# Attention outputs split at query 240 with merged pieces, normalising on VectorE only, the loads of the first batches reordered and one estimate of the kernel's planner raised, in a fused attention and expert kernel

## The chip, the cores and the metric

One core of one Trainium2 chip. The metric is the time of one execution in microseconds, from a timer outside the profile. A profiled execution's span is about 1.7 us shorter than its time. A single-core run carries its mean granted TensorE clock as a share of full speed. A run more than 1.5% above the fastest of its kernel is marked slow and left out of ratios; where one is shown here, it says so.

## The reference, cut to what matters

Eight batches of eight heads, 576 queries, head size 64, with 16 "beacon" keys and values ahead of the 576 causal ones. The attention output, as 4608 tokens of 512, goes through one dense expert.

```python
k_all = np.concatenate([beacon_k, k], axis=2)          # 592 keys
v_all = np.concatenate([beacon_v, v], axis=2)
scores = scale * np.matmul(q, k_all.transpose(0, 1, 3, 2))
scores = np.where(causal, -1e9, scores)                # beacons always visible
a = np.exp(scores - scores.max(-1, keepdims=True))
a /= a.sum(-1, keepdims=True) + 1e-09
x = np.matmul(a, v_all)  # -> (4608, 512)
h = x @ w_in                                           # 512 -> 2048
g = h * (1.0 / (1.0 + np.exp(-1.702 * h)))
out = g @ w_out                                        # 2048 -> 512
```

## The kernel before

The kernel works through 32 attention steps (a pair of heads of one batch; four steps a batch) and nine groups of 512 tokens for the expert. Between attention steps TensorE does expert matmuls, which fill what would be waits for exp on ScalarE. Scores are held with keys on partitions and queries in columns, so the causal part of each of the five key tiles is a rectangle of columns, stored in four chunks:

```python
CH = [[(0, 0, 512)],
      [(0, 512, S), (2, s0s[2], S), (4, s0s[4], S)],
      [(1, s0s[1], S)],
      [(3, s0s[3], S)]]
```

The output of a head is made in two halves of the queries, split at `HS = 288`, each accumulated over key tiles in pieces that follow the chunks:

```python
def av_list(x, half):
    qa, qe = half * HS, (half + 1) * HS
    return [(j, lo - qa, hi - qa, col) for j in range(NJ)
            for (lo, hi, col) in e_pieces(j, max(qa, s0s[j]), qe)]
```

Half of each value tile holds ones, so the sums of exp come out beside the output. After the two copies of a head out of the tiles that TensorE writes (`O<-u`), VectorE transposes the sums (`zt<-O`, one for each head), takes the reciprocal, transposes it back (`rz<-rt`) and multiplies (`xT<-O,rz`, one for each head).

The order of every engine's instructions is computed in the kernel's own Python. Each piece of work carries an estimated duration, for one engine or for a choice of several. A greedy loop repeatedly takes the work that could start earliest by those estimates, picks the engine that would finish it first, and appends it. What comes out is the order of every engine's program. The estimates are typed in by hand:

```python
evs.append(Work(dict(DVE=0.45, ACT=0.46), 0, i + 0.5, ... av_out ...))
zn.append(Work("DVE", 0.68, i + 0.48, lambda i=i, x=x: z_turn(i, x), evs[-2:], ...))   # zt<-O
zr = Work("DVE", 0.2,  i + 0.45, ... z_recip ...)
zk = Work("DVE", 0.75, i + 0.45, ... z_back ...)
nw = Work(dict(DVE=0.78, POOL=1.42), 0, i + 0.45, ... norm ...)                        # xT<-O,rz
...
def issue():                       # cut
    while todo:
        for w in todo:             # skipped while what it needs is not placed
            t = max(end of what it needs + SEM, when its buffer is free)
            eng = min(w.opts, key=lambda e: max(t, free[e]) + w.opts[e] + ...)
            c = (max(t, free[eng]), 0 if same matmul mode else 1, w.key)
            # the smallest c is taken
        free[eng] = w.t0 + w.opts[eng]
        order.append(w)
```

Staging of q and k for batches 2 to 7 goes through two VectorE transposes (`sq<-n`), two copies on VectorE or GpSimd (`t<-sq`), and a pass through DRAM. Batches 0 and 1 are loaded and transposed on TensorE instead.

The softmax here doesn't subtract the row's maximum and nothing guards it: scores larger than these inputs give would overflow.

## Time and profile before

| | before |
|---|---|
| time, median of 3 (range) | 397.88 us (397.56 to 399.22) |
| span of the profiled run | 395.7 us |
| TensorE busy | 368.3 us, 93% |
| VectorE / ScalarE / GpSimd busy | 65% / 57% / 48% |
| five loaded periods (start of one first-expert group to the next) | 41.4, 45.3, 41.4, 42.7, 42.7 us |
| the unloaded period after them | 39.35 us |

The period is the most useful ruler in this kernel: apart from its start and its end it is a loop over batches, and the last of these periods, where nothing is left to stage, shows what the loop takes when TensorE is not kept waiting. From the table of instruction groups of the kernel before, besides what the prediction shows (columns: line, engine, operation, operands, count | busy us, mean ns | idle before them and what ended it):

```profile
L444 DVE STREAM_TRANSPOSE zt<-O 64x576 f32<-64x576 f32 x64 | 49.4, 772 | 1.9
L463 POOL TENSOR_TENSOR xT<-O,rz 64x576 f16<-64x576 f32 x24 | 40.8, 1701 | 71.6 <-DVE rz L454 71.5
L463 DVE TENSOR_TENSOR xT<-O,rz 64x576 f16<-64x576 f32 x40 | 48.8, 1220 | 0.7
```

Set these against the planner's estimates above. The sum transposes take 772 ns where the planner counts 680. The normalisations take 1701 ns on GpSimd (it counts 1420) and 1220 on VectorE (it counts 780). In the 24 pairs that both engines share, VectorE's took 750 ns in the 11 where it started first and 1.41 to 2.52 us in the 13 where GpSimd's did.

### The profile page before, as it was taken

What the parts mean: (1) busy time and instruction counts of PE and PEld (TensorE: products, weight loads), DVE (VectorE), ACT (ScalarE), POOL (GpSimd) and SP (SyncE); (2) the same over time, 40 slices, a digit from 0 to 9 for tenths busy, and PEclk for the clock granted to TensorE, in tenths of its full rate; (3) what the DMA queues carried; (4) which work ended last, traced back from release to release, by engine and by line L of the source; (5) the groups of instructions that cost most, each with busy time, mean ns of one, the idle gap of its engine ahead of it and who ended that gap; (6) DMA issues with size and microseconds to landing.
All of it is one profiled execution on the core that took longest, in us unless ns stands there. A gap on an engine that the chain in (4) does not pass through costs nothing.

```text
span 395.7 us, 6410 instructions
## 1 busy us (share of the span) xinstructions
PE 368.3 (93%) x2458; PEld 186.3 (47%) x2458; DVE 259.0 (65%) x425; ACT 227.3 (57%) x333; POOL 189.1 (48%) x282
## 2 busy tenths in 40 slices
PE   6997999989999799979997999979999999999996
PEld 3464544444544344534453774435454544444442
DVE  6469998699739973999469963997485349000021
ACT  1788766457674656656744766466658563644400
POOL 8664853469255854478337925584355044000000
PEclk9999999999999899999999899999999999999999
DMA  8999994849562795379346966279310010001022
GB/s 114 200 206 208 145 128 132 210 97 154 116 164 60 157 115 132 86 172 124 110 113 145 134 108 146 67 148 120 110 54 30 0 55 27 28 0 53 2 80 80
DMA packets 60894, 42.81 MB, mean 108 GB/s; under 512 B 32192, under 2 KB 53184, under 8 KB 60864
## 3 DMA queue, kind: packets, MB, share of 16 engines
q0 software_dynamic: 42816, 18.62, 38.8%
q1 hardware_dynamic: 18048, 23.79, 18.9%
q8 instruction: 19, 0.31, 0.3%
q14 instruction: 11, 0.09, 0.1%
HBM read 44.40 MB, written 16.61 MB: 154 GB/s over the span
## 4 chain that ended last, share of the span: by engine, by line
PE 50%; DVE 21%; DMA 5%; ACT 4%; issue 2%; POOL 2%; POOLq 1%; DVEq 0%; ACTq 0%
PE u L490 29%; PE u L512 13%; DMA n<-in_k_dram 5%; PE u L421 5%; DVE zt L444 4%; DVE O L432 4%; DVE xT L463 4%; DVE sq L275 4%; PE s L351 2%; ACT E L364 2%; ACT L364 2%; DVE rz L454 2%; DVE t L284 2%; POOL xT L463 1%; POOL t L284 1%
## 5 line engine op out<-in xcount | busy, mean ns | idle before, releaser
L490 PE MATMUL u<-xT,w 128*128 128x512 f16 (+1 forms) x640 | 133.7, 361 | 3.9 <-DVE O L432 1.6
L364 ACT ACTIVATE E<-s 128x1024 f16<-128x1024 f32 (+3 forms) x128 | 104.6, 873 | 49.2 <-PE s L351 45.5
L512 PE MATMUL u<-w,g 128*128 128x512 f16 x576 | 129.4, 379 | 2.3 <-DVE O L432 2.1
L502 ACT ACTIVATE g<-u 128x512 f16<-128x512 f32 x144 | 85.1, 597 | 59.6 <-PE u L490 59.3
L490 PEld LDWEIGHTS <-w 128*128 128x128 f16 x640 | 60.4, 99 | 62.7 <-issue 8.3
L512 PEld LDWEIGHTS <-g 128*128 128x128 f16 x576 | 54.8, 98 | 67.5 <-issue 3.4
L387 POOL TENSOR_SCALAR_AFFINE_SELECT E<-E 128x256 f16<-128x256 f16 (+2 forms) x144 | 58.6, 425 | 42.1 <-ACT E L364 40.8
L463 POOL TENSOR_TENSOR xT<-O,rz 64x576 f16<-64x576 f32 x24 | 40.8, 1701 | 71.6 <-DVE rz L454 71.5
L525 DVE COPY osb<-u 128x512 f32<-128x512 f32 x26 | 17.7, 681 | 76.9 <-PE u L512 76.8
L421 PE MATMUL u<-E,vb 128*128 128x288 f16 (+6 forms) x576 | 58.2, 246 | 7.8 <-POOL E L387 5.7
L432 DVE COPY O<-u 128x288 f32<-128x288 f32 x109 | 45.8, 442 | 27.0 <-PE u L421 26.5
L421 PEld LDWEIGHTS <-vb 128*128 128x128 f16 (+1 forms) x576 | 44.0, 98 | 25.6 <-issue 14.6
L444 DVE STREAM_TRANSPOSE zt<-O 64x576 f32<-64x576 f32 x64 | 49.4, 772 | 1.9
L463 DVE TENSOR_TENSOR xT<-O,rz 64x576 f16<-64x576 f32 x40 | 48.8, 1220 | 0.7
L351 PE MATMUL s<-qT,kT 64*128 64x80 f16 (+5 forms) x384 | 39.9, 286 | 6.1 <-ACT E L364 4.6
L284 POOL COPY t<-sq 128x576 f16<-128x576 f16 x22 | 30.7, 1397 | 26.6 <-DVE sq L275 26.6
L275 DVE STREAM_TRANSPOSE sq<-n 128x576 f16<-128x576 f16 x48 | 35.7, 755 | 4.4 <-DMA n<-in_k_dram 3.8
L351 PEld LDWEIGHTS <-kT 64*128 64x128 f16 x384 | 14.5, 94 | 32.6 <-issue 26.5
L454 DVE STREAM_TRANSPOSE rz<-rt 128x576 f32<-128x576 f32 x32 | 24.4, 762 | 1.3 <-DVE t L290 0.4
L243 POOL DMA_DIRECT2D vb<-in_v_dram x24 | 20.8, 873 | 0.0
L284 DVE COPY t<-sq 128x576 f16<-128x576 f16 x26 | 19.7, 757 | 0.5
L523 ACT COPY osb<-u 128x512 f32<-128x512 f32 x10 | 5.9, 588 | 17.0 <-PE u L512 17.0
(50 smaller groups left out, 147.0 us busy)
## 6 DMA issues: line engine op xcount, KB each, us to landing
out_dram<-osb SPq DMA_DIRECT2D x36, 256.0 KB
d<-t SPq DMA_DIRECT2D x24, 148.0 KB
kT<-d SPq DMA_DIRECT2D x12, 296.0 KB
n<-in_k_dram POOLq DMA_DIRECT2D x12, 288.0 KB, 5.3
n<-in_q_dram POOLq DMA_DIRECT2D x12, 288.0 KB, 6.2
d<-t SPq DMA_DIRECT2D x24, 144.0 KB
qT<-d SPq DMA_DIRECT2D x12, 288.0 KB
vb<-in_v_dram POOLq DMA_DIRECT2D x18, 128.0 KB, 5.5
```

Source lines behind the costliest of these rows:

```text
L275: nc.vector.transpose(sqs[(b, g, w)][:, c * n : (c + 1) * n, :, :], nat[(b, g, w)][:, c * n : (c + 1) * n, :],)
L284: copy[eng](out=tqk[(b, g, w)][:, e, o : o + S].rearrange("p (r t) -> p r t", t=TPP), in_=sqs[(b, g, w)][:, :, e, :].rearrange("p t r -> p ...
L351: nc.tensor.matmul(sc[:, x, o : o + e - a], kT[r : r + 64, p, j * P : (j + 1) * P], qT[r : r + 64, p, a:e], start=True, stop=True,)
L364: nc.scalar.activation(out=Es[i][:, :, choff[ci] : choff[ci] + w], in_=scs[(i, ci)][:, :, 0:w], func=AFT.Exp, scale=0.125,)
L387: nc.gpsimd.affine_select(out=blk, in_=blk, compare_op=ALU.is_ge, fill=0.0, base=mc, pattern=[[0, 2], [1, w]], channel_multiplier=-1,)
L421: nc.tensor.matmul(u[:, lo:hi], vb[0:kw, j, :, :].rearrange("r h c -> r (h c)")[:, o : o + 2 * D], E[0:kw, x, col : col + hi - lo], start= ...
L432: copy[eng](out=Os[i][:, x, half * HS : (half + 1) * HS], in_=avu[(i, x, half)][:, :])
L444: nc.vector.transpose(zst[i][0][64 * x : 64 * x + 64, :, :], Os[i][64 * (1 - x) : 64 * (1 - x) + 64, x, :])
L463: vec[eng].tensor_tensor(out=xT[r : r + 64, p, c : c + S], in0=Os[i][r : r + 64, x, :], in1=zst[i][2][r : r + 64, :], op=ALU.mult,)
L490: nc.tensor.matmul(u[:, o : o + w], w1t[:, kp, nt * P : (nt + 1) * P], xT[:, kp, m : m + w], start=(kp == 0), stop=(kp == NKP - 1),)
L502: nc.scalar.activation(out=gts[g][:, nt, :], in_=hu[(g, nt)][:, :], func=AFT.Gelu_apprx_sigmoid)
L512: nc.tensor.matmul(o[:, :], gts[g][:, nt, mt * P : (mt + 1) * P], w2t[:, nt, :], start=(nt == 0), stop=(nt == NNT - 1),)
```

## The change

The intent: fewer output matmuls (seven pieces a head instead of nine, by a split at query 240, where a chunk boundary of the keys falls, and by merging pieces that lie side by side), no normalising on GpSimd, which takes 1701 ns for one and beside which VectorE's took up to 2.52 us, and earlier loads of v. One more line raises a planner estimate (0.68 to 0.74 for the transpose of the sums). The diff, cut to its core:

```diff
-    HS = S // 2
+    HS = 2 * P - Nb
+    AQ = (0, HS, S)
+    NBV = 2
@@ e_pieces: merge neighbours
-            if lo < hi:
+            if lo < hi and got and got[-1][1] == lo and got[-1][2] + lo - got[-1][0] == col + lo - qa:
+                got[-1] = (got[-1][0], hi, got[-1][2])
+            elif lo < hi:
                 got.append((lo, hi, col + lo - qa))
@@ av_list, av_half, av_out: AQ[half : half + 2] in place of half * HS ...
@@ the first loads (cut)
-    mkeep = Work("POOL", 0.3, 0.0, make_keep)
+    mkeep = Work("POOL", 0.3, -4.75, make_keep)
-        lv = Work("POOL", 0.8, kl + 0.2, lambda b=b: load_v6(b), dma=3.6)
+    def first_values(b):
+        lv = Work("POOL", 0.8, -4.8, lambda b=b: load_v6(b), dma=3.6)
-                            Work("POOL", 0.6, 4.3, lambda x=x: load_bk(x), [V[1, 0]], dma=0.7)
+                            Work("POOL", 0.6, 4.3, lambda x=x: load_bk(x), after=[ld_], dma=0.7)
-            [vpe[NJ - 1], vpe[2 * NJ - 1]][c > 0 :][:1] if c < 3 else [], dma=3.0,
+            vpe[-1:] if 2 * c < 3 * NBV else [], dma=3.0,
+            after=[Lq[(2, 1, 0)]],
@@ the planner's buffer rings: qT, kT, vb as two rings of one instead of one ring of two (cut)
@@ the sum transpose
-                "DVE", 0.68, i + 0.48, lambda i=i, x=x: z_turn(i, x), evs[-2:],
+                "DVE", 0.74, i + 0.48, lambda i=i, x=x: z_turn(i, x), evs[-2:],
@@ the normalisation
-                dict(DVE=0.78, POOL=1.42), 0, i + 0.45, lambda eng, i=i, x=x: norm(i, x, eng),
+                dict(DVE=0.78), 0, i + 0.45, lambda eng, i=i, x=x: norm(i, x, eng),
```

More of the change, by code (lines that the diff above doesn't have):

```diff
@@ L81 @@
     bkn = cst.tile([Nb, NB2, H, D], F16, tag="bkn", name="bkn")
-    bvn = cst.tile([Nb, NB2, H, D], F16, tag="bvn", name="bvn")
+    bvn = cst.tile([Nb, NBV, H, D], F16, tag="bvn", name="bvn")
     def make_keep():
@@ L166, in load_beacons @@
             out=t.rearrange("n b h d -> n (b h) d"),
-            in_=src[0:NB2].rearrange("b h n d -> n (b h) d"),
+            in_=src[0 : t.shape[1]].rearrange("b h n d -> n (b h) d"),
         )
@@ L401, in av_list @@
     def av_list(x, half):
-        qa, qe = half * HS, (half + 1) * HS
+        qa, qe = AQ[half : half + 2]
         return [
@@ L413, in av_half @@
         E = Es[i]
-        u = psu.tile([P, HS], F32, tag="u", name="u")
+        u = psu.tile([P, AQ[half + 1] - AQ[half]], F32, tag="u", name="u")
         avu[(i, x, half)] = u
@@ L432, in av_out @@
         copy[eng](
-            out=Os[i][:, x, half * HS : (half + 1) * HS], in_=avu[(i, x, half)][:, :]
+            out=Os[i][:, x, AQ[half] : AQ[half + 1]], in_=avu[(i, x, half)][:, :]
         )
@@ L552 @@
     rings = dict(
-        n0=2, n1=2, sq=2, t0=2, t1=2, d0=4, d1=4, qT=2, kT=2, vb=2, s=2, E=2, u=4, O=3,
+        n0=2, n1=2, sq=2, t0=2, t1=2, d0=4, d1=4, qT0=1, qT1=1, kT0=1, kT1=1, vb0=1, vb1=1, s=2, E=2, u=4, O=3,
         zt=2, rt=2, rz=2, xT=RING, g=2, osb=3,
@@ L586, in first_loads @@
                     ))
-        lv = Work("POOL", 0.8, kl + 0.2, lambda b=b: load_v6(b), dma=3.6)
-        fb = []
         ub = Buf("u")
@@ L613, in first_loads @@
             kk = 4 * b + 0.5
-            x = Work("PE", 1.35, kk, lambda b=b, j=j: v_pe(b, j), [lv, mspread] + beac[1:], alloc=ub, after=vpe[-1:])
+            x = Work("PE", 1.35, kk, lambda b=b, j=j: v_pe(b, j), [lv, mspread] + beac[1:], alloc=ub,
+                after=vpe[-1:],
+            )
             V[(b, j)] = Work(
@@ L624 @@
     for b in range(B):
-        kTb[b], qTb[b], vbb[b], xTb[b] = Buf("kT"), Buf("qT"), Buf("vb"), Buf("xT")
+        kTb[b], qTb[b], vbb[b] = (Buf(f"{n}{b % 2}") for n in ("kT", "qT", "vb"))
+        xTb[b] = Buf("xT")
         bt = [qTb[b], kTb[b]]
@@ L628 @@
             first_loads(b)
-            continue
-        for g in range(2):
+        for g in range(2) if b >= NB2 else ():
             for w in (1, 0):
@@ L681 @@
                 placed[(b, g, w)] = pl
+        if b < NBV:
+            first_values(b)
+            continue
         for j in range(NJ):
             V[(b, j)] = Work(
-                "POOL", 0.9 + 0.6 * (j == 0), 4 * b - 1.5 + 0.1 * j,
+                "POOL", 0.9 + 0.6 * (j == 0), (4 * b - 1.5 if b >= NB2 else -3.9) + 0.1 * j,
                 lambda b=b, j=j: load_v(b, j, 0, H),
```

## The prediction

> **What bounds the kernel now.** I read the page's engine shares first, then the chain of work that ended last in order of time, then the windows of each stretch between two starts of the first expert matmul, then the waits, and last the timeline around the longest waits of TensorE.
>
> ```profile
> PE 368.3 (93%) x2458; PEld 186.3 (47%) x2458; DVE 259.0 (65%) x425; ACT 227.3 (57%) x333; POOL 189.1 (48%) x282
> ...
> PEclk9999999999999899999999899999999999999999
> ```
>
> TensorE is the bound, but 93% is flattering, since ends are modelled. [...] I took the starts of all matmuls from the trace and listed each gap that exceeds its own columns by over 0.25 us: 29 us, besides 4 us after the last matmul.
>
> ```profile
> 285.95 1.55 PE u L421 x18
> 287.50 0.55 PE s L351 x4
> 288.04 3.56 PE u L512 x16
> 291.60 0.53 PE s L351 x8
> 292.13 1.55 PE u L421 x18
> ```
>
> This is the chain in the seventh batch, where nothing is left to load: one attention step every 6.2 us, all TensorE. In the batches before it the chain leaves TensorE for VectorE and GpSimd. The first expert matmul of each group starts at 88.9, 134.2, 175.5, 218.3, 261.0 and 300.35 us (from the starts). So the periods are 45.3, 41.4, 42.7, 42.7, and 39.35 for the clean one; the period before 88.9 is 41.4. The same stretches as windows (columns: PE, PEld, DVE, ACT, POOL busy, clock, DMA share, GB/s):
>
> ```profile
> 89.00:134.00 45.00, 41.58 (x267) 20.68 (x265) 35.96 (x60) 27.11 (x39) 26.99 (x38) 0.97 0.69 134
> 134.00:175.50 41.50, 39.45 (x250) 19.11 (x248) 32.06 (x55) 26.12 (x38) 24.05 (x35) 0.99 0.66 121
> 175.50:218.30 42.80, 39.86 (x251) 19.16 (x250) 33.58 (x55) 26.50 (x38) 25.61 (x37) 0.98 0.68 127
> 218.30:261.00 42.70, 40.11 (x314) 25.86 (x313) 32.38 (x55) 26.01 (x38) 24.45 (x35) 0.98 0.65 119
> 261.00:300.30 39.30, 38.64 (x248) 18.89 (x246) 29.51 (x49) 24.99 (x38) 22.40 (x33) 1.00 0.50 97
> ```
>
> No other engine is full in any of them (VectorE 76 to 80%), so the 2 to 6 us a period are waits of order. Which ones:
>
> ```profile
> PE u L421 <- POOL E L387: 5.7, 4, 1.5
> ...
> PE s L351 <- ACT E L364: 4.6, 11, 0.5
> ```
>
> The first row is four waits, one a period: the output matmuls wait for a mask on GpSimd. Around one of them:
>
> ```profile
> 130.17 1.16 POOL L284 COPY t<-sq 128x576 f16<-128x576 f16 x1 [2.05 <-DVE sq L275]
> 131.27 0.74 POOL L387 TENSOR_SCALAR_AFFINE_SELECT E<-E 128x256 f16<-128x256 f16 x2
> 131.73 1.79 PE L421 MATMUL u<-E,vb 128*128 128x208 f16 x11 [1.46 <-POOL E L387]
> ```
>
> GpSimd stood 2.05 us waiting for VectorE's staging transpose, copied for 1.16 us, and only then masked what TensorE wanted. [...] The half-clock stretches in the trace (131.7 and 217.0, each 3.4 us) start right after two of these waits.
>
> [...]
>
> ```profile
> 123.78 1.40 POOL L463 TENSOR_TENSOR xT<-O,rz 64x576 f16<-64x576 f32 x1 [1.74 <-DVE rz L454]
> 123.90 1.90 DVE L463 TENSOR_TENSOR xT<-O,rz 64x576 f16<-64x576 f32 x1
> ...
> 334.96 0.75 DVE L463 TENSOR_TENSOR xT<-O,rz 64x576 f16<-64x576 f32 x1
> 335.05 0.81 PE L490 MATMUL u<-xT,w 128*128 128x512 f16 x3
> 335.07 1.90 POOL L463 TENSOR_TENSOR xT<-O,rz 64x576 f16<-64x576 f32 x1 [3.89 <-DVE rz L454]
> ...
> 337.02 0.38 PE L490 MATMUL u<-xT,w 128*128 128x512 f16 x1 [1.17 <-POOL xT L463]
> ```
>
> [...] the free ones here take 750.
>
> **The change part by part.**
>
> 1. Output matmuls. A head had 9 pieces (288, 176, 48; 224, 64, 288, 288, 208, 80 columns) and gets 7 (240, 128; 336, 336, 336, 208, 80); the columns stay 1664. So 128 matmuls go[...]: 0.6 us. [...] The removed quarter of the matmuls is worth next to nothing. The early part also no longer needs the third key tile.
>
> 2. Copies of the outputs. 109 copies of 288 at 0.442 us become 58 of 240 and 45 of 336 on VectorE. [...] these take 0.39 and 0.49 us: 44.8 us for 45.8 (x109 row, "O<-u 128x288"). Six move to ScalarE.
>
> 3. Normalising. 24 of 64 leave GpSimd (1701 ns each, 40.8 us). On VectorE they cost less than their count says. In 13 of the 24 pairs GpSimd was first, and VectorE's own half then took 1.4 to 2.5 us (sum 24.4), in 11 it was free (8.25): 32.6 us. The same pairs on VectorE alone take 24 x 1.51 = 36.2 us, so VectorE pays about 3.6 us in all, and each pair ends about 0.5 us sooner (2.0 to 1.5). Of this only the last pair is on the end's path for certain: 0.5 us.
>
> 4. The order, which moves because the schedule is computed from the part times. The instruction order shows it. In the four periods from 89 us the third step of each batch was torn (scores x2, 16 expert matmuls, scores x4, 3 output matmuls, scores x8, 15 output matmuls), with one staging copy on GpSimd between the masks of one step and another before the next. After, all steps have the pattern of the clean batch (16 expert, 8 scores, 14 outputs, 4 scores), and three of GpSimd's four copies a batch stand after the last mask of the batch. So the mask wait of 1.5 us, the 0.7 us score waits of the torn step and the half-clock stretches (up to 1.7 us each, two of them) should go. The waits that stay: 0.4 us after each table load, which the clean batch has too, and about 1 us behind a staging transpose that stands before three output copies on VectorE (117 us: it waits for its load). That load is issued some 0.7 us sooner without the normalisation ahead of it.
>
> 5. First loads. v of batch 1 goes ahead of its q and k, so these land some 2 to 3 us later (18.0 for the second before). They are first used at 22.6, so no wait. The queue of loads is unbroken to 57 us in both, with the same bytes. w_out comes later in issue but needs to be there at 65.9; I see it landing near 54. The batch-2 loads come some 4 us sooner. The mask constant leaves the end of GpSimd's first queue (VectorE waited 4.5 us for it, TensorE did not). I put the start at -0.5 us.
>
> Sum: five periods of 213.5 us together become five of 40.3, the clean 39.35 plus 0.95 for what stays of the staging waits: 201.5, so -12.0. Start -0.5, end -0.5; part 1 is mostly within the periods. Before 397.9, after near 385.
>
> **Rivals.** (a) VectorE takes the place of GpSimd as what TensorE waits for. A batch's steps with staging hold about 9 us of VectorE work (one 0.69 us output copy, 1.76 us of O copies, two transposes for the sums 1.55, reciprocal 0.25, transpose back 0.76, two norms 1.51, two staging transposes 1.5, a copy 0.76) against 6.2 us of TensorE, and only the first expert layer's stretch lets it catch up. For it: waits for O copies of about 1 us at 81.7 and 117. Against it: 32 to 34 us of work in a 40 us period, no more than before, since the blocked halves vanish. If it comes true the periods are 41 to 41.5 and the time 389 to 391. (b) Only the matmul count matters: then -0.6 us, 397. The torn step and its waits speak against it. (c) The gain goes through fully: periods as the clean one, both half-clock stretches gone, start better by 2: 379 to 381. (d) The late w_out or late q and k of batch 1 stall the start: +2 to +5 us there, visible as DMA waits; the landing times speak against it.
>
> **Range and chances.** I lean to the sum with a part of (a): 385.5, and 8 in 10 between 380.5 and 391.5. The 2% line is 389.9. Faster by over 2%: 0.77; within 2%: 0.21; slower: 0.02, since nothing but the start can lose time.
>
> **What would show it.** Right: the period starts 39.5 to 41 us apart; the wait of outputs for masks near zero; no normalisation on GpSimd, its busy time near 152 us; VectorE's 64 norms at about 0.8 to 0.9 us mean and its busy time 259 to 268; no half-clock stretch inside the periods; output matmuls' full step 1.52 us in the chain instead of 1.55. Wrong: new waits of TensorE for O copies of over 1.5 us a period (rival a), norms of 1.5 us blocked by GpSimd's copies, or DMA waits before 66 us.

## The result, and the profile after

The changed kernel took 385.22 us (median of 4, 382.18 to 386.69), the kernel before 397.99 us in the same rounds (397.56 to 399.22). The ratio is 0.9664, with a 95% interval of 0.9596 to 0.9733: faster by 3.4%. (A ratio here is the mean time of one kernel's fast runs over that of the other's of the same rounds, so not quite the ratio of the medians quoted.) All results agree with the reference.

The page of the changed kernel's profiled execution (386.69 us, the slowest of its four, granted clock 0.985):

```profile
PE 369.8 (96%) x2328; PEld 181.5 (47%) x2328; DVE 265.7 (69%) x443; ACT 226.3 (59%) x334; POOL 146.7 (38%) x263
...
PEclk9789899999999999999999999999999999999999
...
L467 DVE TENSOR_TENSOR xT<-O,rz 64x576 f16<-64x576 f32 x64 | 51.6, 807 | 0.8
```

TensorE's busy time is as before, though 130 matmuls fewer: what went is waiting. Sixty-four normalisations on VectorE take 51.6 us where forty took 48.8. The half-clock stretches (the granted clock is 0.5 in them) stood in the loop before, at 131.7 and 217.0 us; in this run they stand in the start, at 15.0 us (6.83 us long) and 38.9 us (3.41).

The stretches between the starts of the first expert matmuls, now 51.7, 93.9, 133.4, 172.6, 211.8, 251.3 and 290.6 us. The windows below begin with the second loaded period; the first took 42.18 us (columns as in the prediction):

```profile
93.90:133.40 39.50, 38.95 (x235) 18.49 (x234) 34.52 (x59) 25.93 (x38) 19.55 (x34) 1.00 0.72 135
133.40:172.60 39.20, 38.84 (x234) 18.35 (x233) 33.87 (x58) 25.76 (x38) 18.79 (x33) 1.00 0.73 133
172.60:211.80 39.20, 38.84 (x234) 18.42 (x232) 33.05 (x57) 25.76 (x38) 19.23 (x33) 1.00 0.74 134
211.80:251.30 39.50, 39.02 (x298) 24.67 (x296) 33.71 (x59) 25.84 (x38) 18.96 (x33) 1.00 0.75 133
251.30:290.60 39.30, 38.94 (x235) 18.41 (x234) 33.27 (x55) 25.67 (x39) 15.34 (x29) 1.00 0.54 110
```

The loaded periods are now as short as the unloaded one, with a full clock, although VectorE works 33 to 34.5 us in each (85%). Where the gain of the profiled run lies, from these starts:

| part | before | after | difference | predicted |
|---|---|---|---|---|
| start, to the first expert matmul | 47.49 | 51.73 | +4.24 | -0.5 |
| five loaded periods | 213.51 | 199.61 | -13.90 | -12.0 |
| the unloaded period and all after it | 134.70 | 133.66 | -1.04 | -0.5 |
| span | 395.7 | 385.0 | -10.7 | -13.0 |

The waits of TensorE in the changed kernel (engine, tile and line, what it waited for: us in total, times, longest):

```profile
PE s L355 <- ACT E L368: 2.5, 4, 1.0
...
PE u L516 <- DVE O L436: 1.7, 1, 1.7
```

The row "outputs wait for GpSimd's mask: 5.7, 4, 1.5" of before is gone. What replaced it is a single wait of 1.7 us, which ends at 81.4 us.

The chain in the seventh batch, to be held against the one before (outputs x18 in 1.55 us there):

```profile
281.84 0.53 PE s L355 x8
282.37 1.53 PE u L425 x14
283.90 0.56 PE s L355 x4
284.47 3.56 PE u L516 x16
```

Four matmuls fewer in a step shorten it by 0.02 us.

The order on TensorE, one loaded batch, from the traces (number of matmuls; expert1 and expert2 are the matmuls of the first and second expert layer, a bar stands between steps):

```
before: 16 expert2, 8 scores, 18 outputs, 2 scores | 16 expert2, 4 scores, 3 outputs, 8 scores, 15 outputs, 4 scores | 36 expert1 ...
after:  16 expert2, 8 scores, 14 outputs, 4 scores | 16 expert2, 8 scores, 14 outputs, 4 scores | 32 expert1 ...
```

The torn third step of the kernel before, on TensorE (start, us, engine, line, operation; in brackets the idle time before it and its releaser):

```profile
170.63 0.40 PE L421 MATMUL u<-E,vb 128*128 128x288 f16 x3
171.10 0.39 PE L351 MATMUL s<-qT,kT 64*128 64x64 f16 x6
172.01 0.37 PE L351 MATMUL s<-qT,kT 64*128 64x464 f16 x2 [0.53 <-ACT E L364]
172.32 0.54 PE L421 MATMUL u<-E,vb 128*128 128x224 f16 x4
174.19 1.01 PE L421 MATMUL u<-E,vb 128*128 128x208 f16 x11 [1.33 <-POOL E L387]
...
176.79 1.95 PE L490 MATMUL u<-xT,w 128*128 128x512 f16 x7 [0.43 <-DVE xT L463]
```

Outputs and scores alternate with no expert matmuls between them, so each waits for exp or for a mask: 2.3 us of waits in 8 us.

### The profile page after: what moved, and what is told of

Its sections match the earlier page's. It is cut to its first block, busy times and chain, and to the rows that moved or that the text cites.

```text
span 385.0 us, 6119 instructions
## 1 busy us (share of the span) xinstructions
PE 369.8 (96%) x2328; PEld 181.5 (47%) x2328; DVE 265.7 (69%) x443; ACT 226.3 (59%) x334; POOL 146.7 (38%) x263
## 4 chain that ended last, share of the span: by engine, by line
PE 55%; DVE 28%; ACT 7%; DMA 5%; issue 3%; POOL 0%; SPq 0%; ACTq 0%; DVEq 0%
PE u L494 28%; PE u L516 15%; DVE xT L467 6%; DVE zt L448 6%; DVE O L436 5%; PE u L425 5%; ACT E L368 4%; DMA n<-in_k_dram 3%; DVE sq L277 3%; PE s L355 3%; DVE rz L458 3%; PE u L216 2%; ACT L368 2%; PE u L916 2%; DVE osb L529 2%
## 5 line engine op out<-in xcount | busy, mean ns | idle before, releaser
L506 ACT ACTIVATE g<-u 128x512 f16<-128x512 f32 x144 | 83.9, 598 | 52.7 <-PE u L494 52.6
L529 DVE COPY osb<-u 128x512 f32<-128x512 f32 x30 | 20.3, 676 | 74.2 <-PE u L516 74.1
L425 PE MATMUL u<-E,vb 128*128 128x336 f16 (+4 forms) x448 | 57.0, 271 | 0.8 <-DVE qT L187 0.7
L436 DVE COPY O<-u 128x240 f32<-128x240 f32 (+1 forms) x103 | 42.2, 432 | 14.8 <-PE u L425 13.4
L467 DVE TENSOR_TENSOR xT<-O,rz 64x576 f16<-64x576 f32 x64 | 51.6, 807 | 0.8
L425 PEld LDWEIGHTS <-vb 128*128 128x128 f16 (+1 forms) x448 | 39.0, 100 | 20.9 <-issue 4.6
L286 POOL COPY t<-sq 128x576 f16<-128x576 f16 x24 | 29.0, 1208 | 30.8 <-DVE sq L277 30.3
L286 DVE COPY t<-sq 128x576 f16<-128x576 f16 x24 | 26.9, 1121 | 0.2
L216 PE MATMUL u<-w,spread 96*128 96x512 f16 x60 | 16.4, 435 | 0.0
L436 ACT COPY O<-u 128x336 f32<-128x336 f32 (+1 forms) x25 | 10.4, 424 | 2.9 <-PE u L425 2.8
```

The lines of the kernel that those rows point to most:

```text
L286: copy[eng](out=tqk[(b, g, w)][:, e, o : o + S].rearrange("p (r t) -> p r t", t=TPP), in_=sqs[(b, g, w)][:, :, e, :].rearrange("p t r -> p ...
L425: nc.tensor.matmul(u[:, lo:hi], vb[0:kw, j, :, :].rearrange("r h c -> r (h c)")[:, o : o + 2 * D], E[0:kw, x, col : col + hi - lo], start= ...
L436: copy[eng](out=Os[i][:, x, AQ[half] : AQ[half + 1]], in_=avu[(i, x, half)][:, :])
L467: vec[eng].tensor_tensor(out=xT[r : r + 64, p, c : c + S], in0=Os[i][r : r + 64, x, :], in1=zst[i][2][r : r + 64, :], op=ALU.mult,)
L506: nc.scalar.activation(out=gts[g][:, nt, :], in_=hu[(g, nt)][:, :], func=AFT.Gelu_apprx_sigmoid)
```

## The experiments

**Theory** (the prediction's): the order of the torn step is the lever; it moves because the part times moved. **Rivals**: (R1) GpSimd's normalisations are what costs, by their 1701 ns and by VectorE's that take longer beside them (up to 2.52 us for 0.75), whatever the order; (R2) fewer and merged pieces; (R3) the first loads. The diff holds one more candidate, the planner's estimate of the sum transpose, so the first runs take the parts one at a time. "Mean period" below is the mean of the second to the fifth loaded period of the profiled run: 43.03 us before, 39.36 us after. It includes any half-clock stretch inside.

**1. The estimate alone, in the kernel before.** No instruction gets added or removed by this edit; only the planner's opinion changes.

```diff
-                "DVE", 0.68, i + 0.48, lambda i=i, x=x: z_turn(i, x), evs[-2:],
+                "DVE", 0.74, i + 0.48, lambda i=i, x=x: z_turn(i, x), evs[-2:],
```

> The kernel before with one number changed, the planner's estimate of a sum transpose (0.68 to 0.74); both engines may still normalise. It alone mends the torn third step. Theory order (the gain comes from the order of the steps): periods of 40 to 41 us in place of 42.7, 386 to 390 us in all. Rival engine (the gain comes from taking the normalising off GpSimd): within 1% of the kernel before, 394 to 399.

Measured: 385.45 us (382.71 to 387.18), the kernel before 396.36 on this chip, ratio 0.9716 (0.9659 to 0.9773). The mean period is 39.63 us, the third step of the batches is whole, and the mask wait is gone. That is a little faster than the theory's range. One number gives most of the gain; the new one is closer to what the transposes take (772 ns). GpSimd still normalises 24 times, and its share shows in what TensorE now waits for:

```profile
PE u L490 <- POOL xT L463: 2.4, 4, 1.2
...
PE u L490 <- DVE xT L463: 1.7, 2, 0.9
```

**2. Normalising on VectorE only, in the kernel before.**

```diff
-                dict(DVE=0.78, POOL=1.42), 0, i + 0.45, lambda eng, i=i, x=x: norm(i, x, eng),
+                dict(DVE=0.78), 0, i + 0.45, lambda eng, i=i, x=x: norm(i, x, eng),
```

> The kernel before with the normalising on VectorE only; the torn third step stays in the order. Theory order: 392 to 397, the torn step's waits stay. Rival engine: 384 to 388, as the changed kernel.

Measured: 394.03 us (393.14 to 395.0), ratio 0.9937 (0.9889 to 0.9986); mean period 41.57. R1 as the main cause falls: with no normalising left on GpSimd, four fifths of the gain is missing (0.6% against 3.4%). The torn step stays, and TensorE waits for something else in it:

```profile
PE u L490 <- DVE O L432: 8.2, 6, 1.6
```

Instead of GpSimd's masks (5.7 us) it is now VectorE's output copies (8.2 us). Taking away the engine that a wait names did not take away the wait.

**3. The split and the merging alone, in the kernel before** (the HS, AQ, e_pieces and av lines of the diff).

> The kernel before with the outputs split at 240 and the pieces merged, nothing else; the torn step stays. Theory order and my sum: 128 fewer matmuls are worth 0.6 us, and two of the later batches change their order a little: 394 to 398. Rival split (each matmul spared is worth its weight load of about 0.1 us): 385 or less.

Measured: 394.19 us (393.39 to 396.16), ratio 0.9951 (0.9905 to 0.9996); mean period 42.50. R2 falls as the main cause. The mask wait stays (5.6 us in four).

**4. The changed kernel with the old estimate**, the counterpart of run 1.

```diff
-                "DVE", 0.74, i + 0.48, lambda i=i, x=x: z_turn(i, x), evs[-2:],
+                "DVE", 0.68, i + 0.48, lambda i=i, x=x: z_turn(i, x), evs[-2:],
```

> The changed kernel with the planner's old estimate (0.68): split, VectorE normalising and new loads are kept, but the third step is torn again. Theory order: 391 to 396, most of the gain given back. Rival engine: 384 to 387, no change.

Measured: 389.98, 395.27 and 389.95 us, and a slow run of 397.24; ratio of the fast runs 0.9881 (0.98 to 0.9962, called unclear at the 2% line); mean period 41.10. So everything else of the change together gives about 1.2%. Its third step is torn again:

```profile
167.45 0.48 PE L355 MATMUL s<-qT,kT 64*128 64x208 f16 x4
167.86 0.33 PE L425 MATMUL u<-E,vb 128*128 128x240 f16 x2
168.61 0.38 PE L355 MATMUL s<-qT,kT 64*128 64x64 f16 x6 [0.42 <-ACT E L368]
...
172.72 1.46 PE L494 MATMUL u<-xT,w 128*128 128x512 f16 x6 [1.55 <-DVE O L436]
```

This run also explains the spread between runs of one kernel. The runs of 389.95 and 389.98 us had a granted clock of 1.000, that of 395.27 us one of 0.987. A clock of 0.987 over a span of 393 us is 393 x 0.013 = 5.1 us of lost clock, and the two differ by 5.3. I use this below as an estimate: time less (1 - clock) x span.

**5. Estimate and normalising together, in the kernel before**: neither the split nor the loads.

> The kernel before with the new estimate and with the normalising on VectorE only (old split, old loads). With the order mended, theory: the waits of the first expert matmuls for a normalisation on GpSimd (0.6 us a period and 0.9 us before the last two groups in the run with the estimate alone) go: 1 to 4 us under that run, ratio to before 0.962 to 0.970. Rival (VectorE becomes what TensorE waits for): ratio 0.972 or more.

Measured: 381.93 us (380.76 to 385.6), the kernel before 397.31 (396.79 to 403.22, one of them slow), ratio 0.9632 (0.9576 to 0.9687); mean period 39.33. These two lines are the whole gain. From run 1 to this one the ratio goes from 0.9716 to 0.9632; their intervals overlap a little and the chips differ, so the traces are the better evidence. Three places show what normalising on VectorE buys in an order that is whole: 0.3 us a period (39.63 to 39.33), 0.6 us in the unloaded period (39.84 to 39.26), and the stretch from the seventh group's start to the end, 95.36 us in run 1, is 94.44 here, as 94.41 in the changed kernel.

**6. The changed kernel with the old loads** (estimate, normalising and split; the loads, the buffer rings and the mask constant as before).

> The changed kernel with the old first loads and the old buffer model of the planner. If the new loads cost the start (first expert matmul at 51.7 us, against 47.5 before): start near 48 us with the clock at 1.0 there, ratio 0.955 to 0.962. If the late start was the half-clock windows and not the loads: start between 47 and 52 us with the clock's luck, ratio 0.962 to 0.970.

Measured: 382.28 us (379.77 to 383.83), ratio 0.9619 (0.9569 to 0.9668); mean period 39.33. Beside run 5 on the same chip, the split adds nothing that these rounds can see; nor do the new loads in any comparison here, so R3 falls as a source of the gain. The first expert matmul starts at 50.19 us in this run, with the old loads, after two half-clock stretches (16.3 and 36.8 us): a late start does not need the new loads.

**7. The changed kernel with GpSimd allowed to normalise again.**

```diff
-                dict(DVE=0.78), 0, i + 0.45, lambda eng, i=i, x=x: norm(i, x, eng),
+                dict(DVE=0.78, POOL=1.42), 0, i + 0.45, lambda eng, i=i, x=x: norm(i, x, eng),
```

> The changed kernel, but GpSimd may normalise again (23 of 64 go there); order of the steps whole but for one batch. Theory order: ratio 0.968 to 0.975, 1 to 3 us over the changed kernel. Rival engine: ratio 0.985 or more.

Measured: 391.73 us (389.85 to 393.17), ratio 0.987 (0.9819 to 0.9921). My expectation missed, on the slow side. The four later periods are 38.51, 39.27, 39.28 and 39.32 us, quite whole. Of the periods only the first loaded one is longer, 46.78 us against 42.18 in the result's run (43.91 to 44.91 in runs 8 to 10). In it TensorE waits for a copy of expert results, and that copy stands on VectorE behind a staging transpose that waited for its load:

```profile
PE u L425 <- DVE osb L529: 2.9, 1, 2.9
PE u L494 <- POOL xT L467: 2.7, 5, 1.1
```

```profile
81.58 0.78 DVE L277 STREAM_TRANSPOSE sq<-n 128x576 f16<-128x576 f16 x1 [5.07 <-DMA n<-in_k_dram]
...
86.89 0.62 DVE L529 COPY osb<-u 128x512 f32<-128x512 f32 x1
...
87.56 1.24 PE L425 MATMUL u<-E,vb 128*128 128x336 f16 x5 [2.93 <-DVE osb L529]
```

The first row of waits is that one, followed by a half-clock stretch at 87.6 us; the second is what TensorE waited for GpSimd's normalisations directly. The chain that ended last runs through the load itself: 9.99 us on it from issue to landing, against 7.87 in the changed kernel. The timed runs also have lower clocks (0.978 to 0.987). By the estimate of run 4 their time less the lost clock is 384.6 to 385.7 us, against 378.9 to 381.4 for the changed kernel in run 9 (on another chip), so about half of the loss is half clock. How much of the rest is GpSimd's normalising is not shown. Run 1 differs from this kernel only by the old split and the old loads, and its 0.9716 (0.9659 to 0.9773) lies clear of 0.987 (0.9819 to 0.9921): with GpSimd normalising, the new split and loads together cost some 1.5%, half clock included.

**8. The changed kernel with every output piece cut in two**: 896 output matmuls instead of 448, the columns unchanged. It tests the prediction's first part, that the number of output matmuls is worth next to nothing.

```diff
-            nc.tensor.matmul(u[:, lo:hi], ..., E[0:kw, x, col : col + hi - lo], ...)
+            md = lo + (hi - lo) // 2
+            for y, (a0, a1) in enumerate(((lo, md), (md, hi))):
+                nc.tensor.matmul(u[:, a0:a1], ..., E[0:kw, x, col + a0 - lo : col + a1 - lo], ...)
```

> The changed kernel with every output piece cut in two with its own weight load: 896 matmuls in place of 448, the same columns. [...] +1.1 us[...]: ratio to before 0.966 to 0.974. Rival (a weight load shows with its 0.1 us): +45 us. Between: pieces of 60 and 64 columns pay half their weight load, +3 to +8 us.

Measured: 384.46 us (382.72 to 385.67), ratio 0.9676 (0.9639 to 0.9713); mean period 39.37. As expected (0.966 to 0.974). The chain's output step:

```profile
281.14 1.58 PE u L427 x28
```

Fourteen matmuls more took 50 ns more (1534 to 1584 ns to the start of what follows): 3.6 ns each, where the weight load of one takes 100 ns (L425 on the changed kernel's page), so next to nothing of it shows. Cutting the count of output matmuls by a fifth, as the change does, is within the noise, and so is doubling it.

**9. The changed kernel again, five rounds.** The profiled run of the result had 10.2 us of half clock in its start; this asks if that is the kernel's or the run's.

> The changed kernel again, on the chip of the next three, for comparison: ratio 0.962 to 0.970, clocks between 0.985 and 0.995, spread of some 4 us between runs.

Measured: fast runs of 381.14 to 383.66 us, two slow ones of 387.07 and 387.06 (clocks 0.986 and 0.987); ratio 0.9619 (0.9573 to 0.9664). The first expert matmul starts at 46.34 us here, without a half-clock stretch in the start, against 51.73. So the late start was the run's, not the loads'. But the first loaded period is 43.91 us and contains a half-clock stretch at 76.9.

**10 to 12. Holding the clock up.** Thirteen filler matmuls of zeros were added ahead of early score chunks, to keep TensorE from idling in the start, where the half clock stood in the result's run (15.0 and 38.9 us): in the changed kernel (10), in run 6's kernel (11), and in run 5's (12).

```diff
+        for _ in range({(1, 0): 4, (3, 2): 4, (3, 3): 3, (4, 0): 2}.get((i, ci), 0)):
+            warm()
```

> The changed kernel with 13 idle-filling matmuls (4 + 4 + 3 + 2) ahead of the score chunks at which TensorE waited for ScalarE in the start (at 13.8 and 35.8 to 38 us). If the late start is the half clock after those waits: clock 0.993 or more in most runs, 381 to 383 us (ratio 0.957 to 0.963). Rival (the start is late because of ScalarE's chain, the clock doesn't matter): 384 to 387, as the changed kernel.

Measured: 384.04 us (381.55 to 385.36), ratio 0.9652 (0.9607 to 0.9697), so no gain over run 9, and my expectation missed; the number falls in the rival's range. The half clock did stay away from the start (first expert matmul at 47.95 us), but came at 78.9 us, after a wait in the first loaded period, which took 44.34 us.

> As the last, but with the first loads of the kernel before (all other parts of the change kept). If the new loads are worth something: 1 us or more over the last run. If they are worth nothing: within 1 us of it. If they cost the start: under it by 1 us or more.

Measured: 381.4 us (380.55 to 383.95), ratio 0.9612 (0.957 to 0.9653). Its first loaded period is 40.43 us, with no half clock. What differs between 10 and 11 is the loads alone, and the place is a staging transpose on VectorE that waits for its load, with output copies behind it and TensorE behind those. In the changed kernel:

```profile
80.28 0.78 DVE L277 STREAM_TRANSPOSE sq<-n 128x576 f16<-128x576 f16 x1 [2.49 <-DMA n<-in_k_dram]
80.98 1.10 DVE L436 COPY O<-u 128x240 f32<-128x240 f32 x3
81.40 0.81 PE L516 MATMUL u<-w,g 128*128 128x512 f16 x3 [1.73 <-DVE O L436]
```

and in run 11, with the old loads:

```profile
74.57 0.78 DVE L276 STREAM_TRANSPOSE sq<-n 128x576 f16<-128x576 f16 x1 [1.89 <-DMA n<-in_k_dram]
...
75.69 2.53 PE L517 MATMUL u<-w,g 128*128 128x512 f16 x11 [1.12 <-DVE O L437]
```

In run 9 the same wait is 3.06 us on VectorE and 2.31 on TensorE, and there a half-clock stretch follows it. Over all profiled runs with the new estimate, the first loaded period is 42.18, 44.91, 43.91 and 44.34 us with the new loads (the result, runs 8, 9, 10) and 40.85, 41.47, 40.31, 40.43 and 40.86 with the old (runs 1, 5, 6, 11, 12); run 7, with 46.78 us and a wait of 5.07 us at this place, is left out, since GpSimd normalises in it. So the new loads seem to cost 1 to 4 us there, half clock included. The wait itself is not new: VectorE stands idle before this transpose for 1.75 to 2.94 us in the five runs with the old loads, and for 2.49 to 3.68 us in the four with the new. The timed ratios lean the same way (0.9652 against 0.9612), but their intervals overlap, so this is not shown.

> As the last, but with the old split at 288 and 9 pieces a head too, so only the estimate, the VectorE normalising and the fillers are left of the change. [...] 0.6 us over the last run. If the split matters more than that: 2 us or more over it.

Measured: 380.87 us, five runs between 380.71 and 380.99, ratio 0.9585 (0.9549 to 0.9621). This is the kernel before with two planner lines changed and the fillers: every run of it is below every run of the changed kernel in the same rounds (381.14 at best). Its interval of the ratio still overlaps that of run 9 (0.9573 to 0.9664), so it is the best version found, but not one that beats the changed kernel clear of noise. The split left out cost nothing: 0.6 us over run 11 was expected, and the median is 0.5 us under it. What sets run 12 apart is steadiness: its clock was 0.998 to 1.000 in all five runs. By the estimate of run 4, less the lost clock, run 9's four fast runs come to 378.9 to 381.4 us and run 12's to 380.1 to 380.9: no difference left.

| kernel | estimate | normalising | split | loads | median us | ratio of fast runs | mean period |
|---|---|---|---|---|---|---|---|
| before | 0.68 | both | 288 | old | 398.0 | 1 | 43.03 |
| run 2 | 0.68 | VectorE | 288 | old | 394.03 | 0.9937 | 41.57 |
| run 3 | 0.68 | both | 240 | old | 394.19 | 0.9951 | 42.50 |
| run 4 | 0.68 | VectorE | 240 | new | 392.62 (one slow in it) | 0.9881 | 41.10 |
| run 1 | 0.74 | both | 288 | old | 385.45 | 0.9716 | 39.63 |
| run 5 | 0.74 | VectorE | 288 | old | 381.93 | 0.9632 | 39.33 |
| run 6 | 0.74 | VectorE | 240 | old | 382.28 | 0.9619 | 39.33 |
| the change | 0.74 | VectorE | 240 | new | 385.22 | 0.9664 | 39.36 |
| the change, again | 0.74 | VectorE | 240 | new | 383.28 (two slow in it) | 0.9619 | 39.33 |

The three edited kernels at 0.68 lie at 0.988 or above, and all five rows at 0.74 at 0.972 or below. Run 7, which is not in the table, is the exception: at 0.74 and with GpSimd normalising, it has whole later periods, a long first one, lower clocks, and 0.987.

## Why the prediction was right or wrong

The time was right: 385.5 predicted, 385.22 measured, faster by over 2% as given the best chance, and by the mechanism named, a torn step that is made whole. That the total came so close is luck: run 9, the same kernel, has a median of 383.28, and mis-sized terms cancel (below). Point by point:

- **Part 4, the order.** Right in what would happen: periods near 39.4 us, the wait for masks gone, no half clock inside the loop of the profiled run (runs 8 to 10, with the same step whole, have one stretch in the first loaded period). The step that failed is its first clause, that the order "moves because the schedule is computed from the part times", where the only part times it lists are those of removed and resized parts. Runs 2, 3 and 4 have those new part times without the new estimate, and their steps stay torn; run 1 has the estimate alone and is whole. The lever is the number 0.74 for the sum transpose, which stood in the diff and which the prediction's list of parts leaves out. Comparing the orders of the two kernels showed that the order moves, but not which line moves it; building one line at a time would have.
- **The size of the periods.** The term was "40.3, the clean 39.35 plus 0.95 for what stays of the staging waits", five times. The last four measured 39.36 on average, so in them nothing of the 0.95 stayed; the first took 42.18, so there it was nearly three times as much. In sum -13.9 us against -12.0.
- **Part 3, normalising.** Right in its facts (64 at 807 ns; VectorE's busy time 265.7 in the range of 259 to 268; GpSimd 146.7 against near 152). The norms behind GpSimd's copies that it watched for came once in the changed kernel (58.75 us: 1.64 us, over a copy of 1.61), four times before (1.63 to 1.65). The worth of the change of engine beside the order, which the prediction left at 0.5 us for the end, is larger: about 0.9 us at the end, 0.6 in the unloaded period and 0.3 in each loaded one (run 1 to run 5). With the torn order it is worth 43.03 to 41.57 us a period, part of it half clock.
- **Part 1, matmul count.** Right: 1.53 us a step against 1.52 predicted, and run 8 prices a matmul at 3.6 ns. The 0.6 us was the estimate; the outputs of a step, 1550 and 1534 ns at the median in the two traces, give 16 ns a step, 0.5 us in 32.
- **Part 2, copies.** Right: 22.3 + 22.2 us on VectorE against 44.8, and six more on ScalarE. The 0.39 and 0.49 us were the estimate; a straight line through two rows of the table of groups before, copies of 288 columns at 442 ns and of 512 at 681, gives 391 and 493 ns, and the trace of the changed kernel has 384 and 494 ns (58 and 45 copies).
- **Part 5, first loads.** The term -0.5 was +4.24 in the profiled run. Half clock accounts for most of it: 10.2 us of it at a clock of 0.5 is 5.1 us of lost clock, and run 9 started at 46.34. What the prediction did not see is the place where they may cost: it named a wait of VectorE's staging transpose for its load (117 us, about 1 us of TensorE) and expected it to shrink, and in the first loaded period of the changed kernel it is 1.7 to 2.3 us of TensorE.
- **Rival (a), VectorE as the new bound.** It came true in one wait of 1.7 us, not in each period: the last four loaded ones, with VectorE at 85%, took 39.2 to 39.5 us, the unloaded one 39.3.
- **Slips in the working**, without effect on the sum: VectorE fills 75 to 80% of the windows, not 76 to 80; TensorE's wait after a table load for exp, in the clean batch too, is 0.30 us rather than 0.4 (281.59 us, after the load at 278.36).

The clock noise and the two mis-sized terms (start +4.7, periods -1.9, end -0.5 against the prediction) partly cancel, so the total is closer than its parts.

**What stays open.** Why 0.68 tears the step and 0.74 does not is argued only: with 0.68 the planner believes VectorE's queue free earlier than it is, and no run follows the plan decision by decision. The estimate moves the order of every engine at once, and no run moves TensorE's alone. The time with other values is not measured. The planner itself, run without the chip on the kernel before, gives TensorE a whole order in every loaded batch for the values tried from 0.715 to 0.772, and torn third steps at 0.60, 0.62, 0.68 and 0.69; but at 0.64 to 0.67, further from the measured 772 ns, it tears only the first loaded batch. So being nearer to the truth is not shown to be what helps, only that this value does. The estimates for normalising are further off (780 for 1220 ns, 1420 for 1701), and no run corrects them. And whether the new loads cost anything in the time is not settled.

## What to carry to other kernels

Where a program orders itself by estimated durations, compare each estimate with the profile's mean for that group before changing any instruction, and try the order that a better number gives: here 740 in place of 680 ns, where 772 were measured, was worth some 11 us of 396, more than all the changes to the instructions. One such case does not show that a truer estimate is always the better one. A wait names the engine that came last, not the cause: with GpSimd out of the way the same torn order waited for VectorE instead (8.2 us in run 2, for 5.7 on GpSimd before). And with two things changed at once, run each alone, the inconspicuous line first.

## What the traces show of the engines

- TensorE's granted clock: the half-clock stretches lasted 3.41 us (at 131.7 and 217.0 us in the kernel before, at 38.9 in the changed one) or 6.83 us (at 15.0 in the changed one); the last one of each trace, at 394.5 and 383.6 us, is cut off by the end. Within each of the two traces their starts lie whole multiples of 3.413 us apart (25 and 52 of them before, 7 and 101 after). In the kernel before, the 3.41 us ahead of the two stretches of its loop held 2.00 and 1.94 us of TensorE idle time; of the other pieces of 3.41 us between the first and the last matmul, counted from the first stretch, none held more than 1.48. In the changed kernel 0.85 and 1.69 us of idle time stood ahead of its two stretches, and the 1.54 us in the piece from 79.86 us brought none, so the amount alone does not settle it. Ends of matmuls are modelled, so these idle times are too.
- Half clock inside a kernel and repeated timings: one kernel (run 4) ran in 389.95 us at a clock of 1.000 and in 395.27 us at 0.987.
- Matmuls of 512 columns in the expert layers, each with its own weight load (97 to 99 ns), start 216 ns apart at the median of both traces; 16 of them took 3.56 us, with the switch to what follows.
- VectorE's 64 normalisations take 807 ns without GpSimd's, 40 took 1220 ns beside them. Taking them off GpSimd was worth about 0.8% here (run 1 to run 5, whose intervals overlap a little), and the order 2.8% (run 1).
